# A 64x64 merge of the inverse's halves, two heads per product, in a kernel of a recurrence and a mixture

## The chip, the cores and the metric

One core of one Trainium2 chip runs the whole kernel. The metric is the device time of a run in microseconds (us). A profile is one execution of the kernel with every instruction recorded. The engines are named as the profile has them: PE (TensorE, matmuls; PEld is its weight load), DVE (VectorE), ACT (ScalarE), POOL (GpSimd) and SP (which issues most DMAs). [...]

## The reference

Two blocks follow each other. The first is a linear recurrence over 768 steps for 4 batches of 8 heads of 40 columns; the second a mixture of four experts over the 3072 rows that the first gives. All is fp32.

```python
for t in range(S):
    y[:, :, t] = np.einsum('bhd,bhde->bhe', rt, state)
    Sa = np.einsum('bhde,bhe->bhd', state, at)
    state_decay = state * wt[:, :, None, :] - np.einsum('bhd,bhe->bhde', Sa, bt)
    state = state_decay + np.einsum('bhd,bhe->bhde', vt, kt)
...
x = y, as (B*S, H*D)
for e in range(E):
    h = np.maximum(x @ w1[e], 0.0)
    out += p[:, e:e + 1] * (h @ w2[e])
```

## The kernel before

The recurrence is computed in chunks of 64 steps. A unit is one chunk of two batches: 24 units, with 8 heads each, the first batch in partitions 0 to 63 and the second in 64 to 127. Within a chunk, the steps depend on each other through a triangular matrix of 64x64 for each head and batch. Its inverse is needed, and it is made in two steps:

- `substitute` inverts the diagonal blocks of 32x32 by substitution. `blocks` (L516) takes the four diagonal quarters out of F; F (L488) is the copy, made by ACT, of the strictly triangular products `pfe`. DVE turns blocks into M (L519 to L535) and then POOL, in all but the first two units, runs the substitution on Z (L540 to L557), a chain of small operations.
- `merge` turns Z into Qc and QTc (DVE, L568 and L570), has POOL copy the diagonal quarters into QT (L576), and then makes the block off the diagonal from two products: pY from F and QTc (L583), copied by ACT to Yq (L589), and pQ from Qc and Yq (L595), copied by ACT into QT (L600). A quarter is 32 partitions. The block off the diagonal of batch 0 needs quarter 1 of F, that of batch 1 quarter 3; so each product is one matmul of 32 rows, 32 columns and 32 outputs, for each head and batch: 16 for pY and 16 for pQ in a unit.

`within` prepares a unit: the decay G by a scan, the keys and queries, the scores `pc` (L371, through `quadrants`) that DVE copies under a mask into VC (L382), and `pfe`. `step` carries the state on, with `prn`, `psat` (which reads QT), `pxr` and `pdy`; SaT and SX are ACT's copies of psat (L642, L647), RH and SN are the copies of prn. `up` (L726, L734: `ph`) and `products` (L841: `p`) are the mixture; their matmuls fill most of PE's time.

The main loop at the end of the file orders the work by hand, in four parts of a unit (`gap(0)` to `gap(3)`), each of which ends with pieces of the mixture. While unit u is stepped, unit u+1 is merged, and unit u+2 is prepared and substituted. So in PE's queue pY stands after pNT, pKT, pc and prn, and ahead of a ph of the mixture; about 9.7 us of mixture follow, and then come pQ, pfe (of unit u+2) and psat. Instructions marked with `keep_in_program_order` stay in their order on their engine; the others may be moved by a scheduler. On POOL a unit's order is: the QT copies, the start of the next Z, the substitution.

Tiles come from rings. All PSUM (the matmuls' output memory) is in two: `big`, with five buffers of 128x512, from which pg, pNT, pKT, pc, prn, pY, pQ, pfe, psat, pev, pxr and pdy take theirs in turn, and `mm` with three for the mixture. Where a stage uses `banks`, it takes two buffers, one for each half of the array's rows. A matmul that writes a buffer of the ring first waits for the last reader of the tile that held it five tiles earlier.

The lines that matter most:

```python
def big(name):
    return ps.tile([P, 512], FP32, name=name, tag="big", bufs=5)
...
QUADS = ((0, 0), (1, 1), (0, 1), (1, 0))
...
def banks(name):
    return [big(f"{name}{x}") for x in range(2)]
```

Of the kernel before, what the change touches and what calls it, by code (L numbers as in the profile page):

```python
# [7 lines left out]
FP32 = mybir.dt.float32  # L8
# [7 lines left out]
def kernel(  # L16
# [38 lines left out]
    nc = tc.nc  # L55

    B, H, S, D = r.shape
    E, DM, F = moe_w1.shape
    P = 128
    L = 64  # L60
    Q = 32
    NC = S // L
    NJ = H // 2
# [5 lines left out]
    sb = ctx.enter_context(tc.tile_pool(name="sb", bufs=1))  # L69
    ps = ctx.enter_context(tc.tile_pool(name="ps", bufs=1, space=bass.MemoryType.PSUM))  # L70

    def big(name):
        return ps.tile([P, 512], FP32, name=name, tag="big", bufs=5)
# [5 lines left out]
        out=ident[:], in_=ident[:], pattern=[[1, P]], compare_op=ALU.is_equal, fill=0.0,  # L79
# [5 lines left out]
    for t, n, op in ((upf, L, ALU.is_gt), (diagf, Q, ALU.is_equal)):  # L85
        nc.vector.memset(t[:], 1.0)
        for q in range(P // n):
            o = slice(q * n, (q + 1) * n)
            nc.gpsimd.affine_select(
                out=t[o], in_=t[o], pattern=[[1, n]], compare_op=op, fill=0.0, base=0, channel_multiplier=-1,  # L90
# [3 lines left out]
    def dealt(x):  # L94

        return x.rearrange("p h (k g) -> p k g h", g=4)
# [34 lines left out]
    def kept(name, shape, n, value=0.0, eng=nc.gpsimd, lo=0):  # L131
        tiles = []
        for i in range(n):
            t = const.tile(shape, FP32, name=f"{name}{i}")
            eng.memset(t[:, :, lo:shape[2]], value)
            tiles.append(t)
        turn = [0]

        def take():
            turn[0] += 1  # L140
            return tiles[(turn[0] - 1) % n]

        return take
# [7 lines left out]
    for n, a_sum in enumerate(("a1", "a7", "a5", "a2")):  # L151
        t = padded["RV"[n % 2], n // 2] = sb.tile([P, H, 64], FP32, name="padded", tag=a_sum)
# [6 lines left out]
    ETs = kept("ET", of_64, 1)  # L159
    EVs = kept("EV", of_64, 1, lo=D)  # L160
    QTs = kept("QT", of_64, 1)
    RHs = kept("RH", of_64, 1, lo=D)
    state = [kept(f"state{i}_", [P, NJ, 64], 1)() for i in range(B)]

# [151 lines left out]
    def half(s):  # L316
        return slice(64 * s, 64 * s + 64)

    def quarter(q):
        return slice(Q * q, Q * q + Q)  # L320

    def of_slot(x, s):

        return x.rearrange("p (j s) e -> p j s e", s=2)[:, :, s, :]

    def by(x, n):
        return x.rearrange("p (h e) -> p h e", e=n)
# [34 lines left out]
    def banks(name):  # L362
        return [big(f"{name}{x}") for x in range(2)]
# [20 lines left out]
    def within(q):  # L384

        n = q.n
# [9 lines left out]
        for i in range(2):  # L396
# [5 lines left out]
            out=G[:, 0:2 * NJ * L], data0=G[:, 0:2 * NJ * L],  # L402
# [39 lines left out]
        def causal_scores(VT):  # L442
# [8 lines left out]
            out=q.N[:, :, 0:D], in0=n["B"][:], scalar=-1.0, in1=gp[:], op0=ALU.mult, op1=ALU.mult,  # L451
# [25 lines left out]
        p = banks("pfe")  # L477
# [3 lines left out]
        if q.u == 0:  # L481
            p = banks("pe")
        pe = quadrants(p, NJ * L, BY_TOKENS, L, lambda j, s, i: (
            s, i, j, of_pairs(KT, s, j, i), of_slots(q.AT, s, j, i),
        ))
        q.F = sb.tile([P, H, L], FP32, name="F", tag="F", bufs=2)
        for s in range(2):
            nc.scalar.copy(out=of_slot(q.F[:], s), in_=pf[s])  # L488
        yield
# [21 lines left out]
    def substitute(q, eng, between=None):  # L511

        blocks = sb.tile([P, H, Q], FP32, name="blocks")
        for i in range(P // Q):
            move = nc.scalar.copy if i >= 2 else nc.vector.tensor_copy
            tc.keep_in_program_order(move(out=blocks[quarter(i)], in_=q.F[quarter(i), :, quarter(i % 2)]))  # L516
        M = sb.tile([P, Q, Q], FP32, name="M")
        cols = blocks[:].rearrange("p h c -> p c h")[:, :, None, :].to_broadcast([P, Q, 4, H])
        ins = nc.vector.transpose(out=M[:], in_=cols)  # L519
        tc.keep_in_program_order(ins)  # L520


        pairs = M[:].rearrange("p (c two) r -> p c two r", two=2)
        on_diag = M[:].rearrange("p c r -> p (c r)")[:, Q + 1::2 * (Q + 1)]
        tc.keep_in_program_order(nc.vector.memset(on_diag, 0.0))

        Z = sb.tile([P, 4, Q // 4, Q], FP32, name="Z")
        q.Z = Z[:, 0]
        by_second = Z[:, 1:3].rearrange("p x k r -> p (x k) r")
        below = M[:].rearrange("p c r -> p (c r)")[:, 1::2 * (Q + 1)]  # L530
        ins = nc.vector.tensor_tensor(
            out=by_second, in0=pairs[:, :, 1, :], in1=below[:, :, None].to_broadcast([P, Q // 2, Q]), op=ALU.mult,
        )
        tc.keep_in_program_order(ins)
        ins = nc.vector.tensor_tensor(out=pairs[:, :, 0, :], in0=pairs[:, :, 0, :], in1=by_second, op=ALU.add)  # L535
        tc.keep_in_program_order(ins)
        run(between)
        at_once = eng is nc.vector
        for x in (0, 3) if at_once else (0,):
            tc.keep_in_program_order(eng.tensor_copy(out=Z[:, x], in_=unit_cols[:]))  # L540
        for j in range(0, Q, 2):
            n, m = j // 4 + 1, Q - 1 - j
            here = 3 * (j // 2 % 2) if at_once else 0
            ins = eng.tensor_tensor(  # L544
                out=Z[:, 1:3, 0:n, j + 1:Q], in0=M[:, j:j + 2, None, j + 1:Q].to_broadcast([P, 2, n, m]),
                in1=Z[:, here, 0:n, j:j + 2].rearrange("p k x -> p x k")[:, :, :, None].to_broadcast([P, 2, n, m]),
                op=ALU.mult,
            )
            if j == 0:
                tc.keep_in_program_order(ins)  # L550
            z = Z[:, :, 0:n, j + 1:Q]
            if at_once:
                terms = z[:, 0:3] if here == 0 else z[:, 1:4]
                eng.tensor_reduce(out=z[:, 3 - here], in_=terms.rearrange("p x k r -> p k r x"), op=ALU.add, axis=AX.X)
            else:
                for x in range(1, 3):
                    eng.tensor_tensor(out=z[:, 0], in0=z[:, 0], in1=z[:, x], op=ALU.add)  # L557
        if at_once:

            odd, even = (Z[:, x].rearrange("p k (r four) -> p k r four", four=4)[:, :, :, 1:3] for x in (3, 0))  # L560
            eng.tensor_copy(out=even, in_=odd)

    def merge(q):


        Qc = sb.tile([P, H, Q], FP32, name="Qc", tag="q", bufs=2)
        QTc = sb.tile([P, H, Q], FP32, name="QTc", tag="q", bufs=2)
        tc.keep_in_program_order(nc.vector.transpose(out=dealt(Qc[:]), in_=q.Z))  # L568
        tc.keep_in_program_order(
            nc.vector.transpose(  # L570
                out=QTc[:].rearrange("p h r -> p (h r)"), in_=Qc[:].rearrange("p h c -> p (h c)"),
            )
        )
        q.QT = QTs()
        for i in range(P // Q):
            ins = nc.gpsimd.tensor_copy(out=q.QT[quarter(i), :, quarter(i % 2)], in_=QTc[quarter(i)])  # L576
            tc.keep_in_program_order(ins)
        yield

        py = big("pY")  # L580
        for h in range(H):
            for i in (1, 3):
                nc.tensor.matmul(  # L583
                    out=py[quarter(i - 1), h * Q:(h + 1) * Q], lhsT=q.F[quarter(i), h, 0:Q],
                    rhs=QTc[quarter(i), h, :], start=True, stop=True,
                )
        Y = sb.tile([P, H, Q], FP32, name="Yq")
        for i in (0, 2):
            nc.scalar.copy(out=Y[quarter(i)].rearrange("p h t -> p (h t)"), in_=py[quarter(i), 0:H * Q])  # L589
        yield  # L590

        pq = big("pQ")
        for h in range(H):
            for i in (0, 2):
                nc.tensor.matmul(  # L595
                    out=pq[quarter(i), h * Q:(h + 1) * Q], lhsT=Qc[quarter(i), h, :],
                    rhs=Y[quarter(i), h, :], start=True, stop=True,
                )
        for i in (0, 2):
            nc.scalar.copy(out=q.QT[quarter(i), :, quarter(1)], in_=by(pq[quarter(i), 0:H * Q], Q))  # L600
        yield

    def step(q, xT):
# [74 lines left out]
        )  # L678
        Y = sb.tile([P, NJ, 2, L], FP32, name="Y", tag="step", bufs=3)
        Gv = q.G.rearrange("p (j i) t -> p j i t", i=2)  # L680
        for i in range(2):
            nc.vector.tensor_tensor(
                out=Y[:, :, i, :], in0=pdy[i][:, :, D - lo:D - lo + L], in1=(Gv if q.start else RS[:])[:, :, i, :],
                op=ALU.mult if q.start else ALU.add,
            )
        if not q.start:
            nc.vector.tensor_tensor(out=Y[:], in0=Y[:], in1=Gv, op=ALU.mult)
        if not q.end:
# [7 lines left out]
        if placed:  # L696
            px = big("pxT")
            for n, (g, j) in enumerate(PLACES):
                nc.tensor.matmul(
                    out=px[:, g * P:(g + 1) * P], lhsT=pick[:, n, :], rhs=Y[:, j].rearrange("p i t -> p (i t)"),  # L700
                    start=(n == 0 or PLACES[n - 1][0] != g), stop=(n + 1 == len(PLACES) or PLACES[n + 1][0] != g),
# [213 lines left out]
    def run(gen, n=99):  # L915
        if gen is None:
            return
        for _ in range(n):
            if next(gen, gen) is gen:
                break  # L920
# [100 lines left out]
    for u in range(1, NU):  # L1021
        q = units[u]
# [103 lines left out]
```

## Time and profile before

| | |
|---|---|
| median of 3 runs | 1143.27 us (1142.79 to 1145.84) |
| span of the profiled execution | 1139.4 us, of 38243 instructions (its only time on the page) |
| granted TensorE clock, mean | 0.985 |
| matmuls of pY | 768 records in 24 units, 17.0 us busy |
| matmuls of pQ | 768 records, 17.5 us busy |
| ACT's copies to Yq | 48, mean 361 ns |
| ACT's copies of pQ into QT | 48, mean 363 ns |
| POOL's copies of QTc into QT | 96, mean 513 ns |
| DVE's copies into VC | 48, mean 434 ns |

How it is read: busy time of an engine is the time in which at least one of its instructions ran. A product of fp32 leaves two records on PE (so 16 products are 32 records), and matmuls overlap, so that the distance between two starts says more than a record's length. Idle time is put down to the instruction whose end released the waiting one. In the timeline a line is a group of equal instructions that follow each other: its start from the beginning of the span, the length of the group, engine, line, what it writes and reads, and how many.

### The profile page before, as it was taken

The numbers are of one execution on the slowest core, as the hardware profiler recorded it, in microseconds if no ns is written. First come the engines' busy times: TensorE is split into PE (matmuls) and PEld (weight loads), VectorE is DVE, ScalarE is ACT, GpSimd is POOL, SyncE is SP. The second block draws the span as 40 slices with busy tenths as digits, with TensorE's granted clock in tenths as the row PEclk, the third lists the DMA queues.
The fourth block names the chain that finished last, engine by engine and source line by source line (L and its number), as shares of the span: only waits on it lengthen the run. The fifth ranks groups of instructions, "written<-read, shape, count | busy, mean of one in ns | idle before, by whom it ended". The sixth has DMA issues, their size and how long they took to land.

```text
span 1139.4 us, 38243 instructions
## 1 busy us (share of the span) xinstructions
PE 1102.2 (97%) x16036; PEld 979.1 (86%) x16036; DVE 758.5 (67%) x1553; ACT 338.1 (30%) x860; POOL 473.6 (42%) x1221
## 2 busy tenths in 40 slices
PE   6899997999999999999999999999999999999998
PEld 5777776888998989889899898889988898888887
DVE  8766547697767768667677677677677586553343
ACT  2333333333233232332332332332332322311110
POOL 4005626662724635625526526437337246340000
PEclk8899997999999999999999999999999999999999
DMA  7784543255363453544453453443543442231330
GB/s 116 211 245 126 131 101 77 65 109 123 76 148 84 110 127 84 136 119 99 117 121 81 124 117 86 120 101 86 139 101 88 117 110 63 75 90 55 105 92 12
DMA packets 268867, 122.16 MB, mean 107 GB/s; under 512 B 213737, under 2 KB 242073, under 8 KB 268697
## 3 DMA queue, kind: packets, MB, share of 16 engines
q1 hardware_dynamic: 265416, 119.12, 42.7%
q8 instruction: 126, 2.06, 0.8%
q10 hardware_dynamic: 3280, 0.61, 0.3%
q14 instruction: 45, 0.36, 0.1%
HBM read 111.79 MB, written 3.93 MB: 102 GB/s over the span
## 4 chain that ended last, share of the span: by engine, by line
PE 88%; DVE 5%; POOL 2%; issue 2%; ACT 1%; DMA 1%; SPq 1%; DVEq 0%; ACTq 0%; POOLq 0%
PE ph L734 30%; PE p L841 28%; PE ph L726 9%; PE pdy L371 4%; PE po L775 2%; PE pfe L371 2%; PE psat L371 2%; PE pxr L371 2%; PE prn L371 2%; PE pQ L595 1%; PE pc L371 1%; PE pY L583 1%; PE pev L371 1%; POOL Z L557 1%; PE pg L335 1%
## 5 line engine op out<-in xcount | busy, mean ns | idle before, releaser
L734 PE MATMUL ph<-xT,w1p 128*128 128x256 f32 (+1 forms) x1520 | 345.0, 380 | 1.8 <-issue 1.7
L734 PEld LDWEIGHTS ph<-xT,w1p 128*128 128x128 f32 x1520 | 274.7, 191 | 65.3 <-issue 27.0
L544 POOL TENSOR_TENSOR Z<-M,Z 128x62 f32<-128x62 f32 (+7 forms) x352 | 146.7, 417 | 369.1 <-DVE M L535 343.2
L557 POOL TENSOR_TENSOR Z<-Z 128x31 f32<-128x31 f32 (+7 forms) x704 | 255.7, 363 | 55.2
L835 DVE TENSOR_TENSOR a<-hs 128x512 f32<-128x512 f32 x220 | 152.5, 710 | 127.4 <-ACT hs L739 127.4
L739 ACT ACTIVATE hs<-ph 128x512 f32<-128x512 f32 (+1 forms) x208 | 115.8, 564 | 292.3 <-PE ph L734 291.9
L841 PE MATMUL p<-sums,a 128*128 128x160 f32 x1056 | 165.1, 299 | 0.0
L752 DVE SCALAR_TENSOR_TENSOR osb<-p,gate,osb 128x320 f32<-128x320 f32 (+1 forms) x243 | 108.0, 481 | 75.1 <-PE p L841 71.1
L841 PEld LDWEIGHTS p<-sums,a 128*128 128x128 f32 x1056 | 152.9, 190 | 2.3
L726 PE MATMUL ph<-xT,w1p 64*128 64x256 f32 (+1 forms) x760 | 110.0, 398 | 1.5 <-issue 1.4
L841 PE MATMUL p<-w,hs 128*128 128x160 f32 x704 | 102.9, 299 | 0.0
L841 PE MATMUL p<-w,a 128*128 128x160 f32 x704 | 102.9, 299 | 0.0
L841 PEld LDWEIGHTS p<-w,hs 128*128 128x128 f32 x704 | 100.3, 190 | 2.2
L841 PEld LDWEIGHTS p<-w,a 128*128 128x128 f32 x704 | 98.0, 190 | 0.0
L576 POOL COPY QT<-QTc 32x256 f32<-32x256 f32 x96 | 49.3, 513 | 111.6 <-DVE QTc L570 99.9
L726 PEld LDWEIGHTS ph<-xT,w1p 64*128 64x128 f32 x760 | 67.7, 187 | 14.7 <-issue 4.9
L519 DVE STREAM_TRANSPOSE M<-blocks 128x1024 f32<-128x1024 f32 x24 | 47.0, 1957 | 23.1 <-ACT blocks L516 23.0
L414 DVE RECIPROCAL gp<-gp 128x320 f32<-128x320 f32 x24 | 51.7, 2152 | 0.8
L504 ACT COPY EV<-pev 64x160 f32<-64x160 f32 x96 | 23.5, 286 | 67.8 <-PE pev L371 67.4
L371 PE MATMUL pdy<-VC,k_tok 64*64 64x104 f32 (+1 forms) x768 | 41.3, 260 | 0.1
L600 ACT COPY QT<-pQ 32x256 f32<-32x256 f32 x48 | 17.4, 363 | 80.0 <-PE pQ L595 79.4
L626 ACT COPY SN<-prn 128x256 f32<-128x256 f32 x44 | 15.5, 370 | 84.7 <-DVE RH L621 82.3
(148 smaller groups left out, 1369.6 us busy)
## 6 DMA issues: line engine op xcount, KB each, us to landing
w1p<-in_moe_w_dram SPq DMA_DIRECT2D x95, 512.0 KB
w1p<-in_moe_w_dram SPq DMA_DIRECT2D x190, 64.0 KB
w<-in_moe_w_dram SPq DMA_DIRECT2D x4, 1280.0 KB
sums<-in_moe_w_dram SPq DMA_DIRECT2D x9, 512.0 KB
natW<-in_w_dram SPq DMA_DIRECT2D x48, 80.0 KB
natB<-in_b_dram SPq DMA_DIRECT2D x48, 80.0 KB
natK<-in_k_dram SPq DMA_DIRECT2D x48, 80.0 KB
out_dram<-osb SPq DMA_DIRECT2D x46, 80.0 KB
```

Source lines behind the costliest of these rows:

```text
L371: nc.tensor.matmul(out=p[row][half(col), lo + at * out_cols:lo + (at + 1) * out_cols], lhsT=lhsT, rhs=rhs, start=(n == 0), stop=(n == len( ...
L414: pin(nc.vector.reciprocal(out=gp[:], in_=gp[:]))
L519: ins = nc.vector.transpose(out=M[:], in_=cols)
L544: ins = eng.tensor_tensor(out=Z[:, 1:3, 0:n, j + 1:Q], in0=M[:, j:j + 2, None, j + 1:Q].to_broadcast([P, 2, n, m]), in1=Z[:, here, 0:n, j: ...
L557: eng.tensor_tensor(out=z[:, 0], in0=z[:, 0], in1=z[:, x], op=ALU.add)
L576: ins = nc.gpsimd.tensor_copy(out=q.QT[quarter(i), :, quarter(i % 2)], in_=QTc[quarter(i)])
L726: nc.tensor.matmul(out=ph[i][:, f, :], lhsT=w1.last[i * DT:(i + 1) * DT, f, :], rhs=xT[i * DT:(i + 1) * DT, 2, :], start=(f == 0), stop=False,
L734: nc.tensor.matmul(out=ph[i][:, f, :], lhsT=w1.main[:, g, at * P:(at + 1) * P], rhs=xT[:, g, :], start=False, stop=(g == 1 and f == HF // ...
L739: nc.scalar.activation(out=h[:, i * HF // 2:(i + 1) * HF // 2, 0:n], in_=ph[i][:], func=ACTF.Relu,)
L752: nc.vector.scalar_tensor_tensor(out=to, in0=p, scalar=sc, in1=to, op0=ALU.mult, op1=ALU.add)
L835: nc.vector.tensor_tensor(out=t[:], in0=x, in1=y, op=op)
L841: nc.tensor.matmul(out=p[:, n * HD:(n + 1) * HD], lhsT=a[:, f, :], rhs=b[:, f, :], start=(f == 0), stop=(f == HF - 1),)
```

## The change

The products of the merge become matmuls of 64 rows, 64 columns and 64 outputs: two heads are taken side by side, and both quarters of a batch. Of the 64x64 result only the two 32x32 blocks on its diagonal (a head with itself) are used. That the other quarter of the rows adds nothing is had by rows of zeros: `below` holds F's blocks off the diagonal in quarters 1 and 3 and zeros in 0 and 2, and Yq holds its values in quarters 0 and 2 and zeros in 1 and 3. Both are cleared once, at the start; `below` has two buffers in turn, Yq one. POOL fills `below` in `substitute`, right after blocks, with two copies. F, which nothing reads any longer after that, has one buffer in place of two.

There are 8 products each for pY and pQ in a unit, in place of 16. pY takes two buffers of `big`, one for each half of the rows, and its products use all four quadrants of the array; pQ keeps one buffer and uses two quadrants. As the results of the heads lie on diagonals, ACT copies pY in eight pieces (64 columns for each partition) in place of two, and pQ in four (128 columns) in place of two.

```diff
+    Ys = kept("Yq", [P, H, Q], 1)
+    belows = kept("below", [P, H, Q], 2)
...
-        q.F = sb.tile([P, H, L], FP32, name="F", tag="F", bufs=2)
+        q.F = sb.tile([P, H, L], FP32, name="F", tag="F", bufs=1)
...
+        q.below = belows()
+        for i in (1, 3):
+            tc.keep_in_program_order(nc.gpsimd.tensor_copy(out=q.below[quarter(i)], in_=q.F[quarter(i), :, 0:Q]))
         M = sb.tile([P, Q, Q], FP32, name="M")
...
-        py = big("pY")
-        for h in range(H):
-            for i in (1, 3):
-                nc.tensor.matmul(
-                    out=py[quarter(i - 1), h * Q:(h + 1) * Q], lhsT=q.F[quarter(i), h, 0:Q],
-                    rhs=QTc[quarter(i), h, :], start=True, stop=True,
-                )
-        Y = sb.tile([P, H, Q], FP32, name="Yq")
-        for i in (0, 2):
-            nc.scalar.copy(out=Y[quarter(i)].rearrange("p h t -> p (h t)"), in_=py[quarter(i), 0:H * Q])
+        def product(out, lhsT, rhs, r, n):
+            nc.tensor.matmul(
+                out=out[:, n * 2 * Q:(n + 1) * 2 * Q], lhsT=lhsT[half(r), 2 * n:2 * n + 2, :],
+                rhs=rhs[half(r), 2 * n:2 * n + 2, :], start=True, stop=True,
+            )
+
+        def of_two(p, y):
+            return p.rearrange("p (n two t) -> p n two t", two=2, t=Q)[:, :, y, :]
+
+        py = banks("pY")
+        for n in range(NJ):
+            for r in range(2):
+                product(py[r][half(r ^ (n % 2))], q.below, QTc, r, n)
+        Y = Ys()
+        for r in range(2):
+            for x in range(2):
+                for y in range(2):
+                    src = of_two(py[r][quarter(2 * (r ^ x) + y), 0:H * Q], y)
+                    nc.scalar.copy(out=of_slot(Y[quarter(2 * r)], y)[:, x::2, :], in_=src[:, x::2, :])
         yield
 
         pq = big("pQ")
-        for h in range(H):
-            for i in (0, 2):
-                nc.tensor.matmul(
-                    out=pq[quarter(i), h * Q:(h + 1) * Q], lhsT=Qc[quarter(i), h, :],
-                    rhs=Y[quarter(i), h, :], start=True, stop=True,
-                )
-        for i in (0, 2):
-            nc.scalar.copy(out=q.QT[quarter(i), :, quarter(1)], in_=by(pq[quarter(i), 0:H * Q], Q))
+        for n in range(NJ):
+            for r in range(2):
+                product(pq[half(r)], Qc, Y, r, n)
+        for r in range(2):
+            for y in range(2):
+                to = of_slot(q.QT[quarter(2 * r), :, quarter(1)], y)
+                nc.scalar.copy(out=to, in_=of_two(pq[quarter(2 * r + y), 0:H * Q], y))
         yield
```

## The prediction

> **What bounds the kernel now.** First the page: the busy times, the slices, and the chain that ended last.
>
> ```profile
> PE 1102.2 (97%) x16036; PEld 979.1 (86%) x16036; DVE 758.5 (67%) x1553; ACT 338.1 (30%) x860; POOL 473.6 (42%) x1221
> PE   6899997999999999999999999999999999999998
> PE 88%; DVE 5%; POOL 2%; issue 2%; ACT 1%; DMA 1%; SPq 1%; DVEq 0%; ACTq 0%; POOLq 0%
> ```
>
> TensorE (PE) is the bound from about 200 us on[...]. So a matmul taken out saves its time, and a matmul that waits stops the mixture's matmuls behind it. Next the timeline of one unit, around pY (PE, then DVE), and around pQ (PE, then ACT). Columns: start, length, engine and line; in brackets the idle time before and what ended it.
>
> ```profile
> 574.69 0.67 PE L371 MATMUL prn<-ident,state 64*64 64x64 f32 x32
> 575.30 0.69 PE L583 MATMUL pY<-QTc,F 32*32 32x32 f32 x32
> 575.92 1.14 PE L726 MATMUL ph<-xT,w1p 64*128 64x256 f32 x8
> ...
> 571.77 0.63 DVE L568 STREAM_TRANSPOSE Qc<-Z 128x256 f32<-128x256 f32 x1 [1.07 <-POOL Z L557]
> 575.16 1.01 DVE L750 TENSOR_SCALAR osb<-p,gate 128x320 f32<-128x320 f32 x2
> 576.67 0.76 DVE L382 COPY_PREDICATED VC<-mask_up,pc 128x256 f32<-128x256 int32 x2
> ...
> 584.98 0.69 PE L595 MATMUL pQ<-Yq,Qc 32*32 32x32 f32 x32
> 585.61 0.69 PE L371 MATMUL pfe<-NT,AT 64*64 64x64 f32 x32
> 586.12 0.65 PE L371 MATMUL pfe<-AT,KT 64*64 64x64 f32 x32
> 586.59 0.68 PE L371 MATMUL psat<-QT,RH 64*64 64x64 f32 x31
> ...
> 585.72 0.75 ACT L600 COPY QT<-pQ 32x256 f32<-32x256 f32 x2 [4.31 <-PE pQ L595]
> 586.82 0.65 ACT L488 COPY F<-pfe 128x256 f32<-128x256 f32 x2 [0.34 <-PE pfe L371]
> 587.72 0.65 ACT L642 COPY SaT<-psat 128x256 f32<-128x256 f32 x2 [0.25 <-PE psat L371]
> 589.46 0.81 ACT L516 COPY blocks<-F 32x256 f32<-32x256 f32 x2
> ```
>
> See three things. pY takes 0.62 us of PE, pQ 0.63, with no wait. The VC copies, which empty the two banks of pc, run at 576.67, 1.4 us after pY has begun: today nobody cares. And psat begins 0.11 us after the QT copies end (586.47), so that there is no room for a longer copy.
>
> The waits tell what fixes the time of those VC copies:
>
> ```profile
> POOL Z L544 <- DVE M L535: 343.2, 22, 22.8
> DVE Qc L568 <- POOL Z L557: 35.9, 19, 5.2
> DVE M L519 <- ACT blocks L516: 23.0, 16, 3.3
> ```
>
> Blocks (ACT) releases M (DVE), M releases the substitution Z (POOL), Z releases Qc (DVE), and 4.9 us of unbroken DVE work later the first VC copy starts. Ahead of blocks stand SaT and SX, which wait for psat. So the VC copies hang on PE's own pQ and psat of the unit before, and not on a clock of their own.
>
> [...] from one matmul's start to the next it is 38 ns between two 64x64 stages, 148 from 64x64 to 32x32, 121 from 32x32 to 64x64 or to ph, 148 from 64x64 to ph. [...]
>
> **The change, part by part.**
>
> *pY's matmuls.* The steps between starts in the trace: a 32x32 stage begins a pair of matmuls each 32 ns (two tiles at work), a 64x64 stage a group of four each 58 ns (four tiles). Before: 148 + 503 + 121 = 0.77 us from the last prn matmul to ph. After, 8 products on all four quadrants (16 records, two for each fp32 product): 38 + 195 + 148 = 0.38. Saved: 0.39 us a unit, if nothing waits.
>
> *pQ's matmuls.* Two quadrants alone: 8 steps of 58 ns with the usual slow start, 0.44 us, then 38 to pfe, against 503 + 121. Saved: 0.14 us. No stage of before uses just two 64x64 tiles: 0.23 (as with four) to 0.9 us (one after the other, which pairs writing one bank today do not show) bound it.
>
> *The bank.* pY now takes two tiles of big's five. The first falls on pKT's buffer, as now. The second falls on that of pc's second bank, whose reader is the first VC copy; in the built program, pY's second matmul waits for exactly that copy in 17 of the 18 units from the 7th on (before, this wait stood at pQ, 9.7 us later, and cost nothing); in 15 of them the copy ends after pY's start. Behind it on PE stand ph and all the mixture. In the unit shown the first VC copy ends at 576.67 + 0.43 (half of the group's two 434 ns) = 577.10, that is d = 1.81 us after pY's start. Then ph starts at d + 0.10 (semaphore to matmul, as after ACT's copies at 42 us) + 0.20 (the other products) + 0.15 (mode change) instead of at 0.62: a loss of d − 0.17. Read like this in each unit's timeline, in us, from the pY at 311 to that at 927: d = 0.71, 1.68, 3.43, 2.50, 2.21, 2.27, 1.81, 2.23, 2.20, 2.24, 1.87, 2.24, 2.22, 1.24, 2.20; the sum is 31.05, less 15 x 0.17 = **+28.5 us**. At 268 and 971, d is below zero, and the last pY waits for PE alone. Does the wait pay itself off, being met once and not again? No: PE runs later by the stall, but M, Z and VC of the next unit start from pQ and psat after it, so they move along. The distance from pQ's start to the end of the next first VC copy is 36.1 to 36.3 us in ten of the eleven units from 454 to 893. In the units of 311 to 399, M waits for nothing but DVE's own backlog (the sums of weights); there a stall can melt the next one. I take 1.5 off, 4 at most.
>
> *QT in four copies.* ACT's rows: 64x160 takes 286 ns, 64x256 367: 0.84 a column, so 128 columns take some 260. Four with 26 ns between are 1.12 us, for 0.75. They start 0.03 earlier (pQ is shorter by 0.06, its last matmul 27 ns longer) and end 0.34 later, while pfe comes 0.14 earlier. psat's fourth product needs the fourth copy: psat is **0.29 us** later than now, though pQ got cheaper. SaT, SX, blocks, M, Z and VC move with it, so d stays. 17 units have pQ, pfe and psat in a row: **+4.9 us**. Bounds: copies of 230 ns, +2.5; of 300, +8.
>
> *Y in eight copies.* 64 columns: 206 ns by the same slope; eight with gaps 1.85 us, for 0.75. In the units from 268 on pQ comes 9.7 us after pY and SN holds ACT meanwhile: hidden; hs follows at 581.6 where ph is later by 1.6 anyway. In the first units pQ stands one stage behind pY: about 1.1 (unit 0, PE idle there), 0.75, and 0.55 in two others: **+3.0**; at 171 to 200 us PE idles 5.7 us, which may take up 1.
>
> *below, F, POOL.* 48 copies of 32x256; the QT copies from QTc of that size take 513 ns, so 25 us of POOL. They stand ahead of Z, wait for F (ended 2.5 us after pQ's start), and Z's wait for M lasts to 8.9: hidden in the 17 us that POOL waits there. If that cover were gone, 1 us a unit. F with one buffer is read out long before the next unit: nothing. The three memsets are in the start-up's idle POOL: nothing.
>
> *Seven pY without the wait* (four early ones, 268, 971 and the last): 7 x −0.37 = **−2.6**. pQ's saving is inside the term of QT.
>
> Sum: 28.5 − 1.5 + 4.9 + 3.0 − 1.0 − 2.6 = +31.3. On the profiled span of 1139.4: 1171. The page gives no other time for this execution; the median of the runs, 1143.3, lies 3.9 above its span, and so 1143.3 + 31.3 = **1175**.
>
> **The rivals.** (A) *The stall is met once.* If DVE's lag is not renewed in each unit, one stall of 3.4 us puts PE behind it for good: 3.4 + 3.0 + 4.9 − 22 x 0.39 = +2.7: 1146. For it: the units with gapless DVE at 321 to 409. Against it: the constant 36.1 us and M's wait for ACT afterwards. (B) *PE's saving wins.* If the VC copy is done before pY's second matmul, that is d below −0.2 everywhere, and QT's copies are hidden, it is −22 x 0.39 − 17 x 0.14 = −11: 1132. Two units, 268 and 971, are near it; one mechanism, the position of the VC copies in DVE's queue, decides. Fifteen units speak against it. (C) *The loop grows.* The path pQ, psat, blocks, Z, VC, pY, ph becomes the bound, and whatever is added to it (POOL slowed by below's copies, longer ACT copies, pQ's tiles in turn) counts in full: another 0.7 us in 17 units, +12: 1187.
>
> **How the numbers follow.** Forecast 0.80, A 0.07, B 0.05, C 0.08. The forecast's own range: transitional units −2.5 or +1.5, QT −2.4 to +3, the first units ±2, pQ's tiles up to +8: 1168 to 1184. The range reaches up towards C and a little below: 1166 to 1187. What a measurement can tell from no change is 0.3%, 3.4 us: faster takes B, 0.05; A gives half to same, with a scrap of the forecast, 0.04; slower 0.91.
>
> **What would show it.** Right: idle PE before pY of about 2 us, released by DVE VC, in some 15 units; units of about 45.9 us for 43.6; psat waiting on ACT QT by some 0.3 to 0.5 us; PE's busy time less by some 10 us at a longer span; POOL still waiting for M. Wrong: VC copies ending before pY begins, or pY's idle time fading from unit to unit (A).

## The result, and the profile after

| | median | against before (95% interval) | span of the profile | mean granted clock |
|---|---|---|---|---|
| before | 1143.62 us (5 runs) | | 1139.4 us | 0.985 |
| after | 1194.09 us (5 runs, 1191.82 to 1195.31) | 1.0425 (1.0406 to 1.0444) | 1191.6 us | 0.968 |

The change makes the kernel 4.25% slower, some 50 us. The direction was forecast, but the size was not: 1175 was forecast, with 1187 as the upper end of the range.

From the page of the kernel after, the busy times and the chain of waits that ended last:

```profile
PE 1125.9 (94%) x15268; PEld 992.9 (83%) x15268; DVE 767.7 (64%) x1553; ACT 370.7 (31%) x1052; POOL 497.6 (42%) x1272
PE 43%; POOL 24%; DVE 14%; issue 6%; ACT 3%; SPq 1%; DMA 1%; DVEq 0%; POOLq 0%
```

PE ran 768 records fewer, and was busy 23.7 us **longer**. That alone says that something happened to its speed (mean granted clock 0.968 for 0.985), and not only to its waits. PE is no longer the chain's backbone: it fell from 88% to 43%, and POOL and DVE, which were on it with 7%, have 38%.

The timeline of one unit after, around pY: PE, then DVE. The columns are as before.

```profile
592.87 0.67 PE L373 MATMUL prn<-ident,state 64*64 64x64 f32 x32
593.36 0.28 PE L586 MATMUL pY<-QTc,below 64*64 64x64 f32 x2
595.86 0.46 PE L586 MATMUL pY<-QTc,below 64*64 64x64 f32 x14 [2.23 <-DVE VC L384]
596.25 1.93 PE L739 MATMUL ph<-xT,w1p 64*128 64x256 f32 x8
598.11 4.57 PE L747 MATMUL ph<-xT,w1p 128*128 128x256 f32 x16
602.51 1.25 PE L854 MATMUL p<-sums,a 128*128 128x160 f32 x8
...
590.38 0.63 DVE L573 STREAM_TRANSPOSE Qc<-Z 128x256 f32<-128x256 f32 x1 [1.43 <-POOL Z L562]
595.29 0.77 DVE L384 COPY_PREDICATED VC<-mask_up,pc 128x256 f32<-128x256 int32 x2
```

The first product of pY runs (its two records), the second waits 2.23 us for the first of the two VC copies. ph, which reads nothing of pY's, starts only 0.39 us after that second product (596.25): what stands behind the wait in PE's queue waits with it. The forecast had this. But look at the two lines of ph behind it: 1.93 and 4.57 us, where the same lines took 1.14 and 3.72 in the unit shown of before. From ph's start to pQ's it is 10.70 us (596.25 to 606.95), and was 9.06 (575.92 to 584.98). The mixture's matmuls are the same ones, and wait for nothing.

The answer by stretches, of the same unit after: each line has the stretch, its length, the busy time of PE, PEld, DVE, ACT and POOL, and then the granted clock of PE, the DMA's share and GB/s.

```profile
593.36:595.86 2.50, 0.28 (x15) 0.17 (x7) 2.47 (x8) 0.00 (x0) 0.87 (x2) 1.00 0.09 20
595.86:599.86 4.00, 4.00 (x26) 2.85 (x27) 1.95 (x5) 2.29 (x10) 0.00 (x0) 0.57 0.59 171
599.86:606.95 7.09, 7.09 (x45) 6.57 (x45) 3.34 (x6) 1.20 (x2) 0.00 (x0) 1.00 0.78 179
```

In the 4 us after the wait the clock is 0.57 on average. The trace's record of the clock has 0.50 from 596.45 to 599.86, 3.41 us, and 1.00 on both sides; (1 − 0.57) x 4 / 0.5 = 3.4 agrees. The work of 1.7 us is lost in them: the 1.64 us by which ph to pQ is longer. On the page the row of the clock shows nothing but nines from 180 us on, since a slice is 30 us long; a mean of 0.968 for 0.985 is all one sees there.

Last, pQ and the copies of QT in the timeline after, to be laid beside 584.98 to 587.68 of before:

```profile
606.95 0.62 PE L586 MATMUL pQ<-Yq,Qc 64*64 64x64 f32 x13
609.89 1.14 PE L739 MATMUL ph<-xT,w1p 64*128 64x256 f32 x8
607.68 1.10 ACT L613 COPY QT<-pQ 32x128 f32<-32x128 f32 x4 [4.37 <-PE pQ L586]
```

And three lines of the waits (who waited for whom, us in total, times, longest):

```profile
PE pY L586 <- DVE VC L384: 29.2, 13, 2.7
POOL below L521 <- ACT F L490: 286.5, 19, 21.1
POOL Z L549 <- DVE M L540: 105.2, 22, 6.0
```

From pQ to ph it is 2.94 us, for 2.70 before: psat is late by 0.24. POOL still idles before Z (105.2 us in 22 units), so that below's copies are hidden. (The wait for the VC copy is PE's longest one with a known releaser. Its 13 cases are the units from 404 us on. In the two units before, at 315 and 359 us, pY waited too, 0.30 and 1.12 us, and the profile puts it down to POOL's QT copies; there as well the VC copy had ended some 0.15 us before pY went on. So the forecast's 15 units are all there.)

### The profile page after: what moved, and what is told of

It reads as the page before. It is cut to its first block, busy times and chain, and to the rows that moved or that the text cites. A ratio compares the mean times of both kernels' runs of the same rounds, so it can differ in the third digit from the quotient of the medians.

```text
span 1191.6 us, 37012 instructions
## 1 busy us (share of the span) xinstructions
PE 1125.9 (94%) x15268; PEld 992.9 (83%) x15268; DVE 767.7 (64%) x1553; ACT 370.7 (31%) x1052; POOL 497.6 (42%) x1272
## 4 chain that ended last, share of the span: by engine, by line
PE 43%; POOL 24%; DVE 14%; issue 6%; ACT 3%; SPq 1%; DMA 1%; DVEq 0%; POOLq 0%
PE ph L747 15%; POOL Z L562 15%; PE p L854 14%; POOL Z L549 8%; PE ph L739 5%; DVE M L524 3%; PE psat L373 2%; DVE G L403 2%; DVE osb L765 1%; PE po L788 1%; PE pfe L373 1%; SPq L724 1%; ACT SX L660 1%; DVE a L848 1%; PE pdy L373 1%
## 5 line engine op out<-in xcount | busy, mean ns | idle before, releaser
L747 PE MATMUL ph<-xT,w1p 128*128 128x256 f32 (+1 forms) x1520 | 357.7, 390 | 0.0
L747 PEld LDWEIGHTS ph<-xT,w1p 128*128 128x128 f32 x1520 | 284.4, 197 | 68.4 <-issue 28.2
L562 POOL TENSOR_TENSOR Z<-Z 128x31 f32<-128x31 f32 (+7 forms) x704 | 259.2, 368 | 55.2
L549 POOL TENSOR_TENSOR Z<-M,Z 128x62 f32<-128x62 f32 (+7 forms) x352 | 143.7, 408 | 131.0 <-DVE M L540 105.2
L521 POOL COPY below<-F 32x256 f32<-32x256 f32 x48 | 20.8, 434 | 288.1 <-ACT F L490 286.5
L739 PE MATMUL ph<-xT,w1p 64*128 64x256 f32 (+1 forms) x760 | 113.8, 409 | 0.4 <-issue 0.3
L603 ACT COPY Yq<-pY 32x64 f32<-32x64 f32 x192 | 39.2, 204 | 59.4 <-PE pY L586 57.3
L613 ACT COPY QT<-pQ 32x128 f32<-32x128 f32 x96 | 24.7, 258 | 83.9 <-PE pQ L586 82.2
L586 PE MATMUL pY<-QTc,below 64*64 64x64 f32 x384 | 15.7, 229 | 33.5 <-DVE VC L384 29.2
```

The costliest lines, as they stand in the source:

```text
L549: ins = eng.tensor_tensor(out=Z[:, 1:3, 0:n, j + 1:Q], in0=M[:, j:j + 2, None, j + 1:Q].to_broadcast([P, 2, n, m]), in1=Z[:, here, 0:n, j: ...
L739: nc.tensor.matmul(out=ph[i][:, f, :], lhsT=w1.last[i * DT:(i + 1) * DT, f, :], rhs=xT[i * DT:(i + 1) * DT, 2, :], start=(f == 0), stop=False,
L747: nc.tensor.matmul(out=ph[i][:, f, :], lhsT=w1.main[:, g, at * P:(at + 1) * P], rhs=xT[:, g, :], start=False, stop=(g == 1 and f == HF // ...
```

## The experiments

All are against the kernel before, run on the same chip beside them (1143.28 us for four of them, 1144.08 for three; the row "after" is the result above). "A unit" is the distance between the starts of two pQ in the timeline, the most frequent value from 450 us to 970; "stretches" counts the 3.4 us (in one case twice that) at half clock between 270 us and the end of the work, where the kernel before has none. The mean granted clock of the profiled runs goes with them: 0.985 before, 0.968 after, 0.985, 0.982 and 0.971 with 8, 5 and 2 repeats, 0.967 with the bank alone, and 0.986, 0.988 and 0.986 in the last three.

| kernel | median | ratio (95%) | a unit | stretches |
|---|---|---|---|---|
| before | 1143.28 and 1144.08 | | 43.55 to 43.62 | 0 |
| after | 1194.09 | 1.0425 (1.0406 to 1.0444) | 47.6 | 12 |
| with 8 repeats | 1177.09 | 1.0299 (1.0278 to 1.032) | 46.0 | 1 |
| with 5 repeats | 1177.95 | 1.0300 (1.0273 to 1.0327) | 45.95 | 3 |
| with 2 repeats | 1193.68 | 1.0445 (1.0421 to 1.0468) | 47.6 | 11 |
| bank alone | 1196.51 | 1.0464 (1.0441 to 1.0487) | 47.5 | 13 |
| one bank | 1144.22 | 1.0011 (0.9998 to 1.0024) | 43.62 to 43.68 | 0 |
| one bank, pQ as before | 1142.05 | 1.0001 (0.9982 to 1.0020) | 43.38 to 43.44 | 0 |
| pQ alone | 1142.49 | 0.9989 (0.9974 to 1.0003) | 43.79 | 0 |

**PE kept at work in the wait.** The theory: the idle time before pY's second bank costs once as a wait, and once more as a slower clock. So the wait is left as it is, and PE repeats products that it has just made.

```diff
         py = banks("pY")
         for n in range(NJ):
-            for r in range(2):
-                product(py[r][half(r ^ (n % 2))], q.below, QTc, r, n)
+            product(py[0][half(n % 2)], q.below, QTc, 0, n)
+        for _ in range(8 if 9 <= q.u <= 21 else 0):
+            for n in range(NJ):
+                product(py[0][half(n % 2)], q.below, QTc, 0, n)
+        for n in range(NJ):
+            product(py[1][half(1 ^ (n % 2))], q.below, QTc, 1, n)
```

> The changed kernel, with PE kept at work in the wait: pY's four products of the first bank come first, in units 9 to 21 they are repeated eight times (same inputs, same output; about 1.9 us), and then come the four of the second bank, which still wait for the VC copy. Theory (the idle 2.4 us before pY's second product cost twice, once as a wait and once more because PE's clock falls to half for 3.4 us after it): the wait stays, the clock stays at full speed, 12 units lose 1.6 us less: 1174 us (1171 to 1178). Rival (the mixture after pY is longer for another reason, loads of w1p or PE's queue): 1193 to 1196, with ph as slow as in the changed kernel. A third (the repeats add to the time): above 1200.

Measured 1177.09. PE's timeline in this kernel:

```profile
590.89 2.27 PE L586 MATMUL pY<-QTc,below 64*64 64x64 f32 x72
593.38 0.45 PE L586 MATMUL pY<-QTc,below 64*64 64x64 f32 x8 [0.21 <-DVE VC L384]
593.76 1.14 PE L743 MATMUL ph<-xT,w1p 64*128 64x256 f32 x8
594.82 3.72 PE L751 MATMUL ph<-xT,w1p 128*128 128x256 f32 x16
```

And the stretch after the wait (the clock is the number before the last two):

```profile
593.38:597.38 4.00, 4.00 (x28) 3.27 (x29) 1.95 (x5) 2.14 (x10) 0.00 (x0) 1.00 0.55 176
```

pY's second bank still starts 2.49 us after its first, as after the change (593.36 to 595.86). But the clock stays up (1.00 in these 4 us, 0.57 after the change), and ph takes 1.14 and 3.72 as before. 64 useless records in each of 13 units make the kernel 17 us faster. So the second part of the loss is the clock. The kernel is still 33.8 us slower than before, with the wait left as it is; that the wait comes from the bank is tested further down.

**How much idle time does it take?** The same with five and with two repeats:

```diff
-        for _ in range(8 if 9 <= q.u <= 21 else 0):
+        for _ in range(5 if 9 <= q.u <= 21 else 0):
```

```diff
-        for _ in range(8 if 9 <= q.u <= 21 else 0):
+        for _ in range(2 if 9 <= q.u <= 21 else 0):
```

> As the kernel with eight repeats of pY's first products, with five: PE idles about 1.1 us before pY's second bank in place of 0.2. Theory: an idle time so short leaves the clock at full speed, and the wait ends at the same VC copy, so the time is that with eight repeats, 1174 to 1180 us. Rival (the gain of the eight repeats came from something else than idle PE, and grows with them): half way, 1182 to 1188.

> As before, with two repeats: PE idles about 1.75 us. It brackets the idle time from which the clock falls: if it is not reached, 1174 to 1180 us with the clock up; if it is, 1190 to 1197 with half-speed stretches of 3.4 us after the waits, as in the changed kernel. Nothing in between is expected unless only some units fall; I lean to the former (0.6).

The stretch after the wait of one unit with five repeats:

```profile
596.40:600.40 4.00, 4.00 (x28) 3.27 (x29) 1.94 (x5) 2.15 (x10) 0.00 (x0) 1.00 0.44 134
```

PE had idled 0.61 us before it, the shortest of the 11 such waits in this kernel; the others took 0.88 to 0.91 us. After none of them did the clock fall (1.00 in the 4 us shown), and the median is that with eight repeats within 1 us. Of the three stretches at half clock left in this kernel, the first belongs to the unit at 360 us, which has no repeats and a wait of 1.38 us, and the other two follow stops of 1.72 and 1.43 us for which the profile shows no cause. PE's timeline with two repeats:

```profile
599.53 0.45 PE L586 MATMUL pY<-QTc,below 64*64 64x64 f32 x8 [1.58 <-DVE VC L384]
600.98 3.63 PE L751 MATMUL ph<-xT,w1p 128*128 128x256 f32 x8
```

After 1.58 us it falls (0.71 in the 4 us from 599.53, 0.93 in the 7.47 us after those): the first eight records of ph alone take 3.63 us, where sixteen take 3.72 at a clock of 1.00. That kernel is as slow as the one with 2.23 us, although its products come in the same order as those with five and eight repeats; so the order is not what helped. I had leaned to the other outcome (0.6): that lean was wrong. In these two kernels none of the 11 waits of 0.61 to 0.91 us was followed by a fall, and 10 of the 12 of 1.58 to 1.60 us were.

The length of the idle time alone does not tell which waits were hit, though. After the change, the unit at 452 us waited 2.25 us, the next one 2.21, and only the first escaped (clock 1.00 in the 4 us from 454.63, 0.57 in those from 500.62). In the profiles of before and after the trace's record of the clock has the values 1.00 and 0.50 alone, and its changes (8 and 36 stretches) lie whole multiples of 3.413 us apart up to the end of PE's work: a grid that runs through the whole profile. Here the kernel after is cut at the edges of this grid, first around the unit that escaped and then around the next one:

```profile
449.69:453.10 3.41, 2.68 (x108) 2.38 (x105) 3.23 (x10) 1.07 (x2) 2.40 (x4) 1.00 0.09 21
453.10:456.51 3.41, 1.88 (x24) 1.45 (x25) 3.38 (x9) 0.51 (x3) 0.00 (x0) 1.00 0.36 76
497.46:500.88 3.42, 1.21 (x75) 1.10 (x67) 3.39 (x9) 0.00 (x0) 1.53 (x2) 1.00 0.07 16
500.88:504.29 3.41, 3.41 (x24) 2.29 (x15) 1.69 (x4) 2.22 (x10) 0.00 (x0) 0.50 0.58 171
```

An edge cut the first wait into 0.73 and 1.53 us of idle PE, and the clock stayed up. The next wait lay whole in one window, 2.21 us of it, and the window after ran at half clock. From 270 us to the end of PE's work, in these two profiles, each of the 12 windows at full clock in which PE idled 1.66 us or more was followed by one at half clock, and none of those with 1.56 us or less was. In the kernels with repeats it also fell after less: with five after the 1.38 and 1.43 us named above, and with eight after a window with 0.73 us of idle PE, in the unit at 404 us:

```profile
404.76:408.17 3.41, 2.68 (x82) 2.50 (x80) 3.38 (x10) 0.16 (x1) 1.18 (x2) 1.00 0.24 34
408.17:411.58 3.41, 3.41 (x12) 2.32 (x11) 0.03 (x1) 2.00 (x10) 0.00 (x0) 0.50 0.77 229
```

The idle time of a window does not tell it alone either: the window at 404 has the busy time of the one at 449 (2.68 us), and only the former was followed by half clock. Up to 2.08 us of its busy time went to pY's first products and their repeats (404.57 to 406.84). What made the difference is not shown.

**The second bank alone.** The kernel before, with nothing but the ring's second buffer for pY:

```diff
-        py = big("pY")
+        py = banks("pY")
...
-                    out=py[quarter(i - 1), h * Q:(h + 1) * Q], lhsT=q.F[quarter(i), h, 0:Q],
+                    out=py[i // 2][quarter(i - 1), h * Q:(h + 1) * Q], lhsT=q.F[quarter(i), h, 0:Q],
...
-            nc.scalar.copy(out=Y[quarter(i)].rearrange("p h t -> p (h t)"), in_=py[quarter(i), 0:H * Q])
+            nc.scalar.copy(out=Y[quarter(i)].rearrange("p h t -> p (h t)"), in_=py[i // 2][quarter(i), 0:H * Q])
```

> The kernel before, with only one thing of the change: pY takes two banks of the ring (32x32 products and two copies to Yq as before). Theory: the second bank falls on pc's, pY waits for the VC copy in 15 units (31 us) and the clock falls in about 12 of them (20 us): 1194 us (1186 to 1199), as the whole change. Rival (the time lies in the twelve ACT copies, below on POOL or the 64x64 products): 1143 to 1150.

Measured 1196.51: one bank more, without a single new product or copy, does all the harm of the change. PE's timeline in one unit (the only one from 404 us to 980 after which the clock stayed up: 1.00 in the 4 us from 600.10):

```profile
597.77 0.24 PE L583 MATMUL pY<-QTc,F 32*32 32x32 f32 x2
600.04 0.69 PE L583 MATMUL pY<-QTc,F 32*32 32x32 f32 x30 [2.03 <-DVE VC L382]
```

**All of the change but the second bank.** pY's products write one bank, each half of the rows to its own half of the outputs; that leaves two quadrants, and four copies to Yq.

```diff
-        py = banks("pY")
+        py = big("pY")
         for n in range(NJ):
             for r in range(2):
-                product(py[r][half(r ^ (n % 2))], q.below, QTc, r, n)
+                product(py[half(r)], q.below, QTc, r, n)
         Y = Ys()
         for r in range(2):
-            for x in range(2):
-                for y in range(2):
-                    src = of_two(py[r][quarter(2 * (r ^ x) + y), 0:H * Q], y)
-                    nc.scalar.copy(out=of_slot(Y[quarter(2 * r)], y)[:, x::2, :], in_=src[:, x::2, :])
+            for y in range(2):
+                src = of_two(py[quarter(2 * r + y), 0:H * Q], y)
+                nc.scalar.copy(out=of_slot(Y[quarter(2 * r)], y), in_=src)
```

> The changed kernel, with pY's products in one bank (rows r to half r, so two quadrants in place of four) and, since its diagonals then lie together, four copies to Yq in place of eight. below, zero rows and pQ as changed. Theory: no wait on the VC copy, the clock stays up; pY is 0.17 us a unit cheaper than before, psat still late by 0.13 to 0.29: 1143 us (1139 to 1147). Rival (the zero rows, POOL's below or the ACT copies cost by themselves): 1155 or more.

Measured 1144.22, within 0.3% of before: without the second bank the loss is gone. The rows of zeros, below, and the copies leave a unit 0.06 us longer: pY gains 0.17, psat loses 0.24.

**And pQ as before.** To this, pQ's loop and its two copies were put back to those of the kernel before.

```diff
-        for n in range(NJ):
-            for r in range(2):
-                product(pq[half(r)], Qc, Y, r, n)
-        for r in range(2):
-            for y in range(2):
-                to = of_slot(q.QT[quarter(2 * r), :, quarter(1)], y)
-                nc.scalar.copy(out=to, in_=of_two(pq[quarter(2 * r + y), 0:H * Q], y))
+        for h in range(H):
+            for i in (0, 2):
+                nc.tensor.matmul(
+                    out=pq[quarter(i), h * Q:(h + 1) * Q], lhsT=Qc[quarter(i), h, :],
+                    rhs=Y[quarter(i), h, :], start=True, stop=True,
+                )
+        for i in (0, 2):
+            nc.scalar.copy(out=q.QT[quarter(i), :, quarter(1)], in_=by(pq[quarter(i), 0:H * Q], Q))
```

> As the one with one bank, but pQ and its two copies as before (32x32). Theory: pY's 0.17 us a unit stays as a gain, psat is on time again: 1140 us (1138 to 1143), a little faster than before. Rival (psat was not late because of the four copies): the same time as the one with one bank, within 1 us.

PE's timeline around pY in this kernel:

```profile
574.65 0.63 PE L586 MATMUL pY<-QTc,below 64*64 64x64 f32 x16
575.21 1.13 PE L739 MATMUL ph<-xT,w1p 64*128 64x256 f32 x8
```

pY to ph is 0.56 us, for 0.62 before, and from prn's last group to pY it is 0.50 us (574.15 to 574.65), for 0.61 before (574.69 to 575.30): a typical unit is 43.38 to 43.44 us, the 0.17 less that were worked out. The time, 1142.05, lies in the range that was expected, but it is 1.0001 of before, and the gain that was expected is not measured. Its profile has, from 450 us on, three units 1.3 to 3.1 us longer than the rest (45.01, 44.66, 46.47). In the longest, PE stops for 2.8 us in the middle of a group of equal matmuls, where nothing that the profile shows was waited for. The kernel before has such a stop too; its timeline:

```profile
717.81 0.60 PE L371 MATMUL psat<-RH,QT 64*64 64x40 f32 x27
719.97 0.31 PE L371 MATMUL psat<-RH,QT 64*64 64x40 f32 x3 [1.56 <-issue]
```

In the four profiles without the second bank, PE has one to three such stops between 260 and 1115 us, at other places in each: 3.2 us in all in the kernel before, 1.5 with one bank, 5.0 here, and 0.4 in the last kernel below. PE's busy time in the 17 units from 277 us on leaves them out: it is 740.3 us before and 736.9 here. So in these two profiles the stops hide a gain of some 3 us. Whether they also explain why the medians show none is not shown, and no version shown here is faster than before. What the stops are was not looked into.

**pQ alone.** The kernel before, with pQ's products, Yq's rows of zeros and the four copies to QT: the diff above read backwards for pQ (with the helpers that it calls), and

```diff
+    Ys = kept("Yq", [P, H, Q], 1)
...
-        Y = sb.tile([P, H, Q], FP32, name="Yq")
+        Y = Ys()
```

> The kernel before, with pQ's part of the change alone: 64x64 products for two heads, rows of zeros in Yq, four copies into QT; pY as before. Theory: psat is 0.24 us later after pQ's start than before (2.94 for 2.70 from pQ to ph), so 17 units lose that: 1147 us (1144 to 1150), and a unit of 43.8 for 43.6. Rival (pQ's cheaper products win): 1140 to 1142.

The time was missed: 1142.49, where 1144 to 1150 was expected. The unit is what was expected, 43.79 us, 0.24 longer than the shortest of before. But of before's 17 units from 277 us on, several are longer than that (44.30, 44.58, 44.03, 45.56, 44.60) and make its sum 743.8 us; here the sum is 744.3. PE's busy time in these units, which leaves the stops out, is 740.3 us before and 743.7 here. So the loss in each unit is shown, and its effect on the time is not.

## Why the prediction was off

- **The bank and its wait: right.** "pY's second matmul waits for exactly that copy": the timeline has it, the bank alone reproduces it, one bank removes it.
- **That the wait is met anew in each unit: right.** With the clock held up, the units are all 46.0 us long, and the kernel is 33.8 us slower than before; the forecast, which knew nothing of the clock, had said +31.3. Rival A (the stall is met once) would have had 1146. The 1.5 us taken off for the units of 311 to 399 fit too: their VC copies came 0.3 to 0.6 us sooner after pY's start than before.
- **The step that failed** is the price of the wait: "Then ph starts at d + 0.10 … + 0.20 … + 0.15": "a loss of d − 0.17". It takes the work behind the wait to run at its old speed. Instead PE ran at half clock for 3.4 us after 12 of the waits; with the 1.64 us of the unit shown for each, 19.7 us were left out. Add them to +31.3 and the sum is +51.0; the spans differ by 52.2. The kernel before shows half-clock stretches in the first 201 us only, and the chain of the argument had no place for a fall in the midst of the stream. The forecast's own sign for it, "PE's busy time less by some 10 us", was the one that came out the wrong way (+23.7), and its "units of about 45.9 us" are those with the clock held up (46.0), where the change as it stands has 47.65.
- **pY's matmuls: right, but eaten by the wait in most units.** Where pY does not wait after the change, at 271 and 1063 us, ph starts 0.35 and 0.34 us after it, for 0.62 before; with the 0.11 by which prn's last group is nearer to pY (270.90 to 271.40, 0.50 us for 0.61) that is the 0.39 of four quadrants. The 0.17 of two quadrants are there in the units of 43.38.
- **pQ's matmuls and the four copies to QT: right in mechanism, a little smaller.** Copies of 258 ns where 260 had been worked out; psat late by 0.24 in place of 0.29. pQ's 16 records start in pairs, 58 ns from pair to pair after the first two, within 0.46 us (606.95 to 607.41), where one after the other had been bounded at 0.9: two quadrants worked side by side, as taken.
- **The first units: too small, and the cause is open.** The eight copies to Yq took 204 ns each (206 worked out), but pY of the unit at 268 us came at 271.40, later by 3.6 us, where the forecast's terms for the first units leave about 0.5. With the bank alone it is later by 2.0 us, with one bank by 1.8, with pQ alone by 1.2; with one bank and pQ as before, so with four copies to Yq, it is 0.2 us earlier. In these single profiles the bank and pQ's part each cost something there, and four copies to Yq nothing that shows. The half-clock stretches of the start-up lie elsewhere in each kernel, and the shares were not separated.
- **below, F's one buffer, POOL: right,** hidden in POOL's wait for M (105 us of it are left).

## What to carry to other kernels

A stage that takes one more buffer out of a shared ring takes it from a certain earlier tile: look up which, and when its last reader ends, before counting what the stage saves. A wait in the midst of a matmul stream may have to be priced twice, as idle time and as slow matmuls after it (here stretches of 3.4 us at a clock of 0.50 came after waits of 1.58 to 2.66 us); ask for the granted clock in windows of a few us, as a mean over the kernel hides it (0.968 for 0.985). A cheaper product whose results lie scattered pays in copies, and where these copies release the next stage, they are on the path even if their engine is 31% busy (here four copies of 258 ns for two of 363, and psat 0.24 us late).

## What the runs showed of the hardware

Waits of 1.58 to 1.60 us in a stream that was otherwise full were followed by 3.4 us of PE at half clock in 10 of the 12 units of one run (two repeats); the 11 waits of 0.61 to 0.91 us of another (five repeats) never were. In the profiles of before and after, the changes of the clock lie on a grid of 3.413 us, and from 270 us to the end of PE's work the half-clock windows are those that come after a window with 1.66 us or more of idle PE (12 of 12; none after 1.56 us or less). With five repeats the clock also fell after 1.38 and 1.43 us, and with eight after 0.73 us. Filling the wait with useless products of 64x64 bought 17 us of 1194.

After the change, the unit's length of 47.65 us is nearly 14 windows (14 x 3.413 = 47.79), so that the wait comes back at nearly the same place of a window each time. From 498 us on the half-clock stretches begin every 47.79 us (at 500.88, 548.66 and so on up to 978.74), first 0.26 us after the end of the wait and at the last 1.44 us after it. So most of each wait lay in one window (1.87 to 2.28 us of it), and 11 units in a row were hit.
